# A decode step on one core: TensorE work as register loops, row slices on their own partitions, and 8 KB reads of w2 and wo

## The chip, the core and the metric

The kernel runs on one core of a Trainium2 chip. The metric is the device time of one execution in microseconds (us), lower is better. The two executions of the kernel before that are compared with the change took 104.36 and 104.44 us.

## The reference, cut to what matters

It is one token of a decoder layer with a parallel MLP: normalize the row `x` (1024), do sliding-window attention over the last 4096 cached keys, do an MLP on the normalized row, and add everything.

```python
xn = layernorm(x)                                   # x: 1 x 1024, bf16
q  = xn @ wq                                        # wq 1024 x 4096 -> 32 heads of 128
p  = softmax(q . k_window * 128**-0.5)              # 4 KV heads, window 4096, 8 query heads each
o  = p @ v_window                                   # "P.V" below
h  = gelu(layernorm(xn) @ w1 + b1)                  # w1 1024 x 3584
out = x + o @ wo + h @ w2 + b2                      # wo 4096 x 1024, w2 3584 x 1024
# (cut: the original writes these as two functions with einsum)
```

About 39.85 MB have to be read from memory for some matrix-vector products. So reading is one floor. The other is TensorE: wq, w1, w2 and wo are used as the moving operand (the one that streams past the stationary one), 512 columns at a time, 64 + 56 + 56 + 64 = 240 matmuls. A "piece" below is one of the transfers, mostly of about 1 MB, in which a matrix is read.

## The kernel before

It is a fully unrolled program. Each vector that multiplies a matrix is one stationary column, so each result is a row on one partition, spread over several banks of the accumulator. The row is copied to the on-chip memory (SBUF) and turned back into columns by one-column transposes.

```python
# q: one output row, eight banks on one partition
pe.matmul(PS[0:1, n*512:(n+1)*512], lhsT=XNTb[:, k:k+1],
          rhs=WA[:, k*NQ + n*512 : k*NQ + (n+1)*512], ...)
# ... copies of that row: 2048 columns on one partition, DVE and ACT, then 32 of these:
last = pe.matmul(PSb[:, 6*1024 + 2*h : ...+1], lhsT=Qrow[0:1, h*128:(h+1)*128],
                 rhs=identb[0:1, 0:1], is_transpose=True)
# K is transposed by TensorE (128 transposes), then 128 score matmuls of 8 columns.
# P.V: V is stationary, 8 probability columns move
for g in range(HKV):
    for b in range(NBLK):                       # 32 blocks
        pe.matmul(PS[:, 2048 + g*8 : ...+8], lhsT=V[:, (g*NBLK+b)*128 : ...+128],
                  rhs=Pb[:, (g*NBLK+b)*8 : ...+8], start=(b == 0), stop=(b == NBLK-1))
# ... w2 and wo accumulate into the same row
W2_CHUNKS = [9, 9, 8, 2]                        # rows of 2 KB per partition: runs of 18, 18, 16, 4 KB
sp.dma_start(WA[...].rearrange("p (h n) -> p h n", h=nh),      # wo: runs of 2 KB
             A_wo[h0*128:(h0+nh)*128, :].rearrange("(h d) n -> d h n", h=nh))
for h in range(32):
    for n in range(2):
        pe.matmul(PS[0:1, 3072+n*512 : ...], lhsT=OT[:, h:h+1],
                  rhs=WA[:, h*D+n*512 : ...], start=False, stop=(h == 31))
```

The order of the big reads is wq, w1, K, V, w2, wo. The matmuls of w2, P·V and wo come last.

## Time and profile before

| | before |
|---|---|
| time, median of 2 runs | 104.4 us (104.36 to 104.44) |
| span in the trace | 102.4 us |
| TensorE busy | 81.3 us |
| last wo piece landed (the trace's landing records) | 98.8 us |
| TensorE ends | 100.1 us |

The span, from the first to the last instruction of the program, is 2 us shorter than the time. First, the four rows of the page that show it in 40 slices of 2.56 us. Busy shares and clock (PEclk, the share of TensorE's full clock that was granted) are in tenths, 9 is 90% or more; GB/s is what the DMA engines moved.

```profile
PE   0021899999559998849999856489999999999991
...
PEclk9999999999999999995999955559995999999999
DMA  2999999999999999999999999999999999999910
GB/s 38 406 414 426 426 438 416 426 426 431 420 434 421 423 417 433 432 435 413 422 422 419 416 457 396 461 461 408 416 373 408 403 408 410 407 410 410 366 54 1
```

The queue is busy from the second slice to the third from last, and TensorE is at 9 in the twelve slices before the last. Where wo is read in runs of 2 KB (from about 78 us on, the 31st to 37th slice) the rate is 403 to 410 GB/s; it was 406 to 438 in the first half, apart from the first slice. The end of the chain of waits (start, duration, what; all in us) shows who closes the kernel:

```profile
43.18 23.65 DMA W<-in_B_w_dram
66.83 0.14 issue
66.96 5.34 PE PS L409 x18
...
72.37 3.30 PE PS L578 x128
...
76.00 9.98 PE PS L409 x38
85.98 12.22 PE PS L633 x56
...
98.24 1.90 PE PS L633 x8
```

Up to 66.83 us the chain is DMA; then TensorE runs w2 (L409), P·V (L578, 128 matmuls in 3.30 us) and wo (L633) without a gap to 98.20 us. Only at its last 8 matmuls does TensorE meet the last two pieces of wo, which landed at 98.2 and 98.8 us. So two limits end within 2 us of each other, and a change that relieves only one gains little.

### The profile page before, as it was taken

The page shows a single profiled execution, that of the slowest core. Times are in us where ns is not written, and L with a number is a line of the kernel's source. Part 1 is how long each engine was busy: PE and PEld are TensorE (multiplying, and loading weights), DVE is VectorE, ACT ScalarE, POOL GpSimd, SP SyncE. Part 2 cuts the span into 40 slices and gives each one's busy share as a digit, 9 for nine tenths or more (in the row PEclk, how much of TensorE's full clock was granted, in tenths as well). Part 3 has the DMA queues.
Part 4 walks back from the last instruction along what each step waited for, and adds up shares of the span by engine and source line. Part 5 has one row for each costly group of instructions (what it writes and reads, how often), then busy time and mean ns, then how long its engine had stood idle before and what let it go on. Part 6 is the DMA issues. An engine that isn't in the chain of part 4 may idle for free.

```text
span 102.4 us, 1568 instructions
## 1 busy us (share of the span) xinstructions
PE 81.3 (79%) x700; PEld 41.1 (40%) x700; DVE 22.0 (21%) x47; ACT 14.1 (14%) x16; POOL 3.5 (3%) x14
## 2 busy tenths in 40 slices
PE   0021899999559998849999856489999999999991
PEld 0020333333123331339999753023872333333320
DVE  0016400000440000074759444540110000000002
ACT  5000510000420000053337400300000000000002
POOL 5700000000000000000000000000000000000000
PEclk9999999999999999995999955559995999999999
DMA  2999999999999999999999999999999999999910
GB/s 38 406 414 426 426 438 416 426 426 431 420 434 421 423 417 433 432 435 413 422 422 419 416 457 396 461 461 408 416 373 408 403 408 410 407 410 410 366 54 1
DMA packets 8407, 39.95 MB, mean 390 GB/s; under 512 B 721, under 2 KB 721, under 8 KB 5970
## 3 DMA queue, kind: packets, MB, share of 16 engines
q1 hardware_dynamic: 8274, 39.85, 94.5%
q8 instruction: 5, 0.08, 0.3%
q0 software_dynamic: 128, 0.01, 0.1%
HBM read 39.86 MB, written 0.00 MB: 389 GB/s over the span
## 4 chain that ended last, share of the span: by engine, by line
DMA 49%; PE 34%; SPq 14%; issue 1%; DVE 1%
DMA W<-in_B_w_dram 49%; PE PS L409 15%; PE PS L633 14%; SPq L160 10%; SPq L157 4%; PE PS L578 3%; PE PS L310 2%; DVE ROW L650 1%; PE PS L588 0%; PE PS L562 0%
## 5 line engine op out<-in xcount | busy, mean ns | idle before, releaser
L409 PE MATMUL PS<-W,GT 128*1 128x512 bf16 x56 | 15.4, 443 | 1.9 <-DMA W<-in_B_w_dram 1.9
L283 PE MATMUL PS<-WA,XNTb 128*1 128x512 bf16 x64 | 16.0, 417 | 0.3 <-DVE msy L244 0.3
L310 PE MATMUL PS<-W,YTb 128*1 128x512 bf16 x56 | 12.7, 379 | 3.5 <-DVE ROW L293 2.4
L633 PE MATMUL PS<-WA,OT 128*1 128x512 bf16 x64 | 14.3, 379 | 0.0
L439 PE MATMUL PS<-identb,KV 128*128 128x128 bf16 x128 | 9.1, 243 | 1.5 <-ACT ROW L336 1.5
L409 PEld LDWEIGHTS PS<-W,GT 128*1 128x1 bf16 x56 | 5.2, 95 | 12.1 <-issue 7.3
L283 PEld LDWEIGHTS PS<-WA,XNTb 128*1 128x1 bf16 x64 | 5.7, 90 | 10.2 <-issue 2.9
L439 PEld LDWEIGHTS PS<-identb,KV 128*128 128x128 bf16 x128 | 8.8, 111 | 1.6 <-ACT ROW L336 1.6
L310 PEld LDWEIGHTS PS<-W,YTb 128*1 128x1 bf16 x56 | 4.4, 83 | 11.9 <-DVE ROW L293 2.9
L633 PEld LDWEIGHTS PS<-WA,OT 128*1 128x1 bf16 x64 | 5.2, 84 | 8.9 <-DMA WA<-in_A_wo_dram 1.0
L454 DVE COPY KV<-PS 128x1024 bf16<-128x1024 bf16 x10 | 6.3, 685 | 2.3 <-PE PS L439 2.3
L466 ACT ACTIVATE KV<-PS 128x1024 bf16<-128x1024 bf16 x6 | 5.9, 1019 | 3.3 <-PE PS L439 3.3
L650 DVE CAST ROW<-PS 1x512 bf16<-1x512 f32 x1 | 0.7, 678 | 23.6 <-PE PS L633 23.6
L293 DVE CAST ROW<-PS 1x2048 bf16<-1x2048 f32 x1 | 2.3, 2278 | 14.8 <-PE PS L283 14.8
L177 PE MATMUL PS<-identb,X 8*128 8x8 bf16 x1 | 0.2, 181 | 6.5 <-DMA X<-in_A_x_dram 6.5
L644 ACT ACTIVATE ROW<-PS 1x512 bf16<-1x512 f32 x1 | 0.6, 586 | 34.3 <-PE PS L633 34.3
L298 ACT ACTIVATE ROW<-PS 1x2048 bf16<-1x2048 f32 x1 | 1.9, 1866 | 13.8 <-PE PS L283 13.8
L480 PE MATMUL PS<-QT,KV 128*128 128x8 bf16 x128 | 3.4, 167 | 0.4 <-DVE KV L454 0.4
L480 PEld LDWEIGHTS PS<-QT,KV 128*128 128x128 bf16 x128 | 3.3, 98 | 0.6 <-DVE KV L454 0.6
L336 ACT ACTIVATE ROW<-PS 1x1536 bf16<-1x1536 f32 x1 | 1.4, 1439 | 15.3 <-PE PS L323 15.3
L331 DVE COPY QT<-PS 128x32 bf16<-128x32 bf16 x1 | 0.2, 192 | 14.8 <-PE PS L323 14.8
L578 PE MATMUL PS<-Pb,KV 128*128 128x8 bf16 x128 | 3.4, 166 | 0.0
(77 smaller groups left out, 37.8 us busy)
## 6 DMA issues: line engine op xcount, KB each, us to landing
WA<-in_A_wq_dram SPq DMA_DIRECT2D x8, 1024.0 KB, 11.7
W<-in_B_w_dram SPq DMA_DIRECT2D x8, 896.0 KB, 25.4
WA<-in_A_wo_dram SPq DMA_DIRECT2D x7, 1024.0 KB, 15.1
W<-in_B_w_dram SPq DMA_DIRECT2D x2, 2304.0 KB, 26.2
KV<-in_A_k_cache_dram SPq DMA_DIRECT2D x4, 1024.0 KB, 26.2
KV<-in_A_v_cache_dram SPq DMA_DIRECT2D x4, 1024.0 KB, 27.1
W<-in_B_w_dram SPq DMA_DIRECT2D x1, 2048.0 KB, 33.1
WA<-in_A_wo_dram SPq DMA_DIRECT2D x1, 768.0 KB, 12.7
```

Source lines behind the costliest of these rows:

```text
L157: sp.dma_start(WA[:, k * NQ:(k + 1) * NQ], A_wq[k * 128:(k + 1) * 128, :]).then_inc(s_wq[k], 16)
L160: sp.dma_start(W1[:, k * F:(k + 1) * F], B_w1[k * 128:(k + 1) * 128, :]).then_inc(s_w1[k], 16)
L283: last = pe.matmul(PS[0:1, n * 512:(n + 1) * 512], lhsT=XNTb[:, k:k + 1], rhs=WA[:, k * NQ + n * 512: k * NQ + (n + 1) * 512], start=(k == ...
L293: STATE["d_qrow0"] = DVE.mark(dve.tensor_copy(Qrow[:, 0:2048], PS[0:1, 0:2048]))
L310: last = pe.matmul(PS[0:1, (n + 1) * 512:(n + 2) * 512], lhsT=YTb[:, k:k + 1], rhs=W1[:, k * F + n * 512: k * F + (n + 1) * 512], start=(k ...
L409: pe.matmul(PS[0:1, 6 * 512 + n * 512: 6 * 512 + (n + 1) * 512], lhsT=GT[:, c:c + 1], rhs=reg[:, n * 512:(n + 1) * 512], start=False, stop ...
L439: last = pe.matmul(PSb[:, col0: col0 + 128], lhsT=KT[:, g * W + b * 128: g * W + (b + 1) * 128], rhs=identb[:, :], is_transpose=True)
L454: last = dve.tensor_copy(KT[:, g * W + (hu * 16 + 8 * s_) * 128: g * W + (hu * 16 + 8 * s_ + 8) * 128], PSb[:, bk * 1024:(bk + 1) * 1024])
L466: STATE["a_ktcopy"][u] = ACT.mark(act.activation(out=KT[:, g * W + (hu * 16 + 8) * 128: g * W + (hu * 16 + 16) * 128], in_=PSb[:, bk * 102 ...
L480: last = pe.matmul(PS[:, bank_base + b * 8: bank_base + (b + 1) * 8], lhsT=KT[:, g * W + b * 128: g * W + (b + 1) * 128], rhs=QT[:, g * 8: ...
L578: last = pe.matmul(PS[:, 4 * 512 + g * REP: 4 * 512 + (g + 1) * REP], lhsT=V[:, (g * NBLK + b) * DH:(g * NBLK + b + 1) * DH], rhs=Pb[:, (g ...
L633: last = pe.matmul(PS[0:1, 6 * 512 + n * 512: 6 * 512 + (n + 1) * 512], lhsT=OT[:, h:h + 1], rhs=WA[:, h * D + n * 512: h * D + (n + 1) * ...
```

## The change

The intent: fewer instructions and wider work outside the matrix products. A row result is no longer on one partition. For q, h and out, each 512-column slice gets its own partition: the stationary operand is a window of a zero-padded tile, so that the vector stands in column n and zeros elsewhere, and all slices accumulate in one bank. That makes the copy 512 columns wide and the turn-around four transposes instead of 32. K is transposed by VectorE, and P·V has 32 matmuls of 512 columns. w2 and wo are stored four rows per partition, so that one run is 8 KB. The TensorE program is written as loops whose addresses and waits use registers; for such a wait GpSimd counts the landed pieces of each matrix into one semaphore. The order of reads becomes wq, K, V, w1, w2, wo.

```diff
 # q (w1 likewise with YZ, 13 columns per k and 7 slices)
-    pe.matmul(PS[0:1, n*512:(n+1)*512], lhsT=XNTb[:, k:k+1], rhs=WA[...])
+    with pe.Fori(0, KC) as k:
+        pe.wait_ge(r_wq, k + 1)                  # a count that GpSimd forwards
+        for n in range(NWQ):
+            last = pe.matmul(bank(2, 512, 8),
+                lhsT=XZ[:, bass.ds(k * 15 + (7 - n), 8)],
+                rhs=WA[:, bass.ds(k * NQ + n * 512, 512)], start=False, stop=False)
 # K
-    last = pe.matmul(PSb[...], lhsT=KT[...], rhs=identb[:, :], is_transpose=True)   # x128
+    dve.transpose(KT(g).rearrange("p (b t i) -> p t b i", b=4, t=T), K(g))          # x4
 # P.V
-    last = pe.matmul(PS[..., 8 columns], lhsT=V[... 128 columns], rhs=Pb[... 8 columns])  # x128
+    with pe.Fori(0, T // 4) as t:
+        for u in range(4):
+            last = pe.matmul(
+                bank(2, 512, 32), lhsT=PT[:, bass.ds(t * 128 + u * 32, 32)],
+                rhs=Vt[:, bass.ds(t * 4 + u, 1), :, :], start=False, stop=False)
 # w2 (wo likewise with OZ, WA, r_wo and 7 passes; its eighth part stays unrolled)
-    pe.matmul(PS[0:1, ...], lhsT=GT[:, c:c+1], rhs=reg[:, n*512:(n+1)*512])
+    with pe.Fori(0, NH) as n:
+        pe.wait_ge(r_w2, n + 1)
+        for e in range(4):
+            for hf in range(2):
+                pe.matmul(bank(6, 512, 2),
+                          lhsT=GZ[:, bass.ds(n * 12 + (e * 3 + 1 - hf), 2)],
+                          rhs=W2[:, bass.ds(n * 4096 + (e * D + hf * 512), 512)],
+                          start=False, stop=False)
 # the reads
-    w2_pcn = B_w2.rearrange("(p c) n -> p c n", c=FC)        # 9, 9, 8, 2 rows a piece
+    w2_n = B_w2.rearrange("(n p e) d -> n p (e d)", p=128, e=4)
+    wo_n = A_wo.rearrange("(n p e) d -> n p (e d)", p=128, e=4)
 # (cut: set-up, layer norms, softmax with one maximum per row, gelu, forwarding on GpSimd)
```

## The prediction

> **What bounds it now.** The span is 102.4 us (the page); the measured time is 2.0 us more. In the slices all DMA engines are busy from about 2.5 to 95 us, moving 39.85 MB at 405 to 438 GB/s. The chain of waits runs over DMA to 66.8 us (w2's landing), then over TensorE without a gap to 98.2 us: 18 w2 matmuls, P·V 3.3 us, 38 w2 matmuls 9.98 us, 56 wo matmuls 12.22 us, so 218 ns per 512-column matmul at full clock. It then waits for the last wo piece, works 1.9 us, copies and stores (about 2.3 us). Queue and TensorE finish within a few us of each other. Two stretches at half clock (59 to 70 and 77 to 81 us, the clock row) cost TensorE about 3.5 us there.

> **What changes.** Bytes stay. wo goes from 2 KB to 8 KB pieces: the last slices run at 405 to 410 GB/s, the 8 KB stages at about 425; over 8.4 MB that saves about 1 us. The order becomes wq, k, v, w1, w2, wo. From before's landings (15.7 MB by 41.4 us) I put w1's last piece (24.1 MB) at 60.6 us, wo's last at 96 to 97. K is transposed on VectorE instead of TensorE[...]. Gone: one-partition copies of 2.3, 1.9 and 1.4 us, 60 one-column transposes. Scores and P·V become 32 matmuls of 512 columns each instead of 128 of 8 (3.4 us): P·V is now 7.0 us.

> **Critical path.** After h, in TensorE's order: copy and transposes, P·V (34 matmuls), w2 (56), o rearranged (estimate 2.2 us), wo (64): 154 matmuls. At 218 ns that is 33.6 us. From h ready at 62.3: 62.3+1.7+33.6+2.5 = 100.1 us, then 2.5 us to the end: span 102.6, time about 104.5, no gain, though DMA alone would allow 100.5. TensorE closes the kernel.

> **Predicted time** 107 us, 80% range 102 to 120. Faster by over 2%: 0.14; within 2%: 0.37; slower: 0.49.

> **What would show it.** DMA busy to about 96 us, then a TensorE tail of several us, wo loop without DMA waits. Start-to-start of matmuls in the w2 and wo loops: 218 is array-bound, more is sequencer-bound.[...]

> **What would make it wrong.** Loops hidden and h earlier than 61 us: 101 to 102. Register work dearer[...]: 120 or more. Half clock in the w2 loop: +3 us.

The sum under "Critical path" comes to 104.5 us; the 107 us add 2.5 us for the loops. The marked passages are cut. The time of a transpose on VectorE, and what was worked out from it, is in no term of the sum. The price of one looped matmul on the sequencer was the ground for the 2.5 us; it is the "it" of "Up to 218 it is hidden". The 1.7, 2.2 and 2.5 us of that paragraph are estimates; for o rearranged, 1.74 us (u_all) to 2.18 us (u_w2) were measured (table below).

## The result

| | before | after |
|---|---|---|
| time, median | 104.4 us | 113.44 us (113.12 to 113.76, 2 runs) |
| span | 102.4 us | 111.8 us |
| ratio, 95% interval | | 1.087 (1.079 to 1.095): slower |
| last wo piece landed | 98.8 us | 99.5 us |
| TensorE ends | 100.1 us | 109.6 us |

A ratio here and below is the mean time of one kernel's fast runs over the mean of the other's in the same rounds, so it is not quite the ratio of the medians.

The same rows of the page after (slices of 2.8 us):

```profile
PE   0279998773099563857999989888999894999992
...
PEclk9999999999656999655599999999999999999999
DMA  2999999999999999999999999999999999900000
GB/s 42 409 422 431 428 422 422 422 416 419 419 422 419 419 422 417 418 423 416 418 418 421 422 422 422 419 419 419 419 410 422 419 419 413 364 11 0 0 0 1
```

The queue is idle in the last five slices and TensorE is not: TensorE alone closes the kernel, 10 us after the last byte. That much the prediction had said. TensorE has no clock trouble in these last stages, and yet its row shows 8 where the work is dense. The groups of the page (line, engine, operation, count, busy us and mean ns of one, then idle time before them and its releaser) say where:

```profile
L340 DVE STREAM_TRANSPOSE BIG<-BIG 128x4096 bf16<-128x4096 bf16 x4 | 17.8, 4446 | 18.1 <-DMA BIG<-in_A_k_cache_dram 17.8
...
L414 PE MATMUL PS<-BIG,YZ 128*7 x56 | 14.4, 425 | 0.0
L525 PE MATMUL PS<-BIG,GZ 128*2 x56 | 13.2, 378 | 1.1 <-issue 1.1
...
L447 PE MATMUL PS<-BIG,WA 128*32 x32 | 8.9, 379 | 1.7 <-issue 1.5
```

"issue" is time in which the engine waited for nothing that the profile shows. It stands before the loops of w2 (L525) and P·V (L447), not before the loop of w1 (L414). (The mean of one matmul, 378 ns for w2, is its whole duration and overlaps the next; the time from start to start, 215 to 216 ns inside a pass of w2, is the better measure of pace.) The timeline of TensorE from P·V on, some rows of it (start, duration, what, count, idle before):

```profile
67.67 2.29 PE L447 MATMUL PS<-BIG,WA 128*32 x8
70.21 1.14 PE L447 MATMUL PS<-BIG,WA 128*32 x4 [0.25 <-issue]
71.59 1.12 PE L447 MATMUL PS<-BIG,WA 128*32 x4 [0.25 <-issue]
...
78.59 1.90 PE L525 MATMUL PS<-BIG,GZ 128*2 x8
80.65 1.89 PE L525 MATMUL PS<-BIG,GZ 128*2 x8 [0.15 <-issue]
82.76 1.89 PE L525 MATMUL PS<-BIG,GZ 128*2 x8 [0.22 <-issue]
...
95.04 12.81 PE L562 MATMUL PS<-WA,OZ 128*2 x56 [0.79 <-DVE OZ L551]
107.69 1.89 PE L572 MATMUL PS<-WA,OZ 128*2 128x512 bf16 x8
```

A pass is one run through the body of a loop; its boundary is the time from the start of its last matmul to the start of the first of the next pass. Every pass of P·V (4 matmuls) and of w2 (8 matmuls) is followed by a gap. After the first pass, the matmuls inside a pass of P·V start 245 to 270 ns apart, inside a pass of w2 or wo 215 to 216 ns apart. The boundary is 622 to 663 ns in P·V, 531 to 630 in w2 and 297 to 343 in wo. So no single price per matmul describes it.

### The profile page after: what moved, and what is told of

The parts are those of the page before. It is cut to its first block, busy times and chain, and to the rows that moved or that the text cites. A ratio compares the mean times of both kernels' runs of the same rounds, so it can differ in the third digit from the quotient of the medians.

```text
span 111.8 us, 1419 instructions
## 1 busy us (share of the span) xinstructions
PE 86.7 (78%) x346; PEld 30.6 (27%) x346; DVE 29.1 (26%) x38; ACT 10.7 (10%) x27; POOL 4.3 (4%) x20
## 3 DMA queue, kind: packets, MB, share of 16 engines
q1 hardware_dynamic: 5904, 39.85, 86.4%
## 4 chain that ended last, share of the span: by engine, by line
PE 52%; DMA 19%; DVE 18%; issue 4%; SPq 3%; ACT 2%; DVEq 0%
DMA BIG<-in_A_k_cache_dram 19%; DVE BIG L340 16%; PE PS L414 13%; PE PS L525 12%; PE PS L562 11%; PE PS L447 8%; SPq L171 3%; PE PS L352 3%; PE PS L572 2%; DVE MX L366 1%; ACT R L424 1%; ACT R L538 1%; ACT OR L580 1%; PE PS L388 1%; PE PS L356 0%
## 5 line engine op out<-in xcount | busy, mean ns | idle before, releaser
L340 DVE STREAM_TRANSPOSE BIG<-BIG 128x4096 bf16<-128x4096 bf16 x4 | 17.8, 4446 | 18.1 <-DMA BIG<-in_A_k_cache_dram 17.8
L298 PE MATMUL PS<-WA,XZ 128*8 x64 | 16.3, 414 | 1.5 <-POOLq L215 1.5
L352 PE MATMUL PS<-BIG,QBD 128*128 x32 | 11.4, 478 | 4.5 <-DVE BIG L340 3.3
L414 PE MATMUL PS<-BIG,YZ 128*7 x56 | 14.4, 425 | 0.0
L525 PE MATMUL PS<-BIG,GZ 128*2 x56 | 13.2, 378 | 1.1 <-issue 1.1
L562 PE MATMUL PS<-WA,OZ 128*2 x56 | 12.8, 378 | 0.8 <-DVE OZ L551 0.8
L447 PE MATMUL PS<-BIG,WA 128*32 x32 | 8.9, 379 | 1.7 <-issue 1.5
L298 PEld LDWEIGHTS PS<-WA,XZ 128*8 x64 | 5.8, 92 | 12.4 <-issue 6.5
L414 PEld LDWEIGHTS PS<-BIG,YZ 128*7 x56 | 5.3, 95 | 8.6 <-issue 3.1
L525 PEld LDWEIGHTS PS<-BIG,GZ 128*2 x56 | 4.6, 81 | 9.3 <-issue 4.4
L562 PEld LDWEIGHTS PS<-WA,OZ 128*2 x56 | 4.6, 82 | 8.6 <-issue 3.3
L447 PEld LDWEIGHTS PS<-BIG,WA 128*32 x32 | 2.9, 92 | 7.6 <-issue 6.7
## 6 DMA issues: line engine op xcount, KB each, us to landing
WA<-in_A_wq_dram SPq DMA_DIRECT2D x8, 1024.0 KB, 12.2
```

Source lines behind the costliest of these rows:

```text
L298: last = pe.matmul(bank(2, 512, 8), lhsT=XZ[:, bass.ds(k * 15 + (7 - n), 8)], rhs=WA[:, bass.ds(k * NQ + n * 512, 512)], start=False, stop ...
L340: dve.transpose(KT(g).rearrange("p (b t i) -> p t b i", b=4, t=T), K(g)).then_inc(S_KT, 1)
L352: last = pe.matmul(bank(hf), lhsT=QBD[:, bass.ds(k * 128, 128)], rhs=BIG[:, bass.ds(k * 1024 + (kt0 + hf * 512), 512)], start=False, stop= ...
L414: last = pe.matmul(bank(5, 512, NW1), lhsT=YZ[:, bass.ds(k * 13 + (6 - n), NW1)], rhs=W1[:, bass.ds(k * F + n * 512, 512)], start=False, s ...
L447: last = pe.matmul(bank(2, 512, 32), lhsT=PT[:, bass.ds(t * 128 + u * 32, 32)], rhs=Vt[:, bass.ds(t * 4 + u, 1), :, :], start=False, stop= ...
L525: pe.matmul(bank(6, 512, 2), lhsT=GZ[:, bass.ds(n * 12 + (e * 3 + 1 - hf), 2)], rhs=W2[:, bass.ds(n * 4096 + (e * D + hf * 512), 512)], st ...
```

## The experiments

**How the theories stood.** The main theory: TensorE's instruction sequencer, which has to run the register instructions of a loop, sets the pace where the loops are not paced by anything else. Rivals: the zero-padded operands or the shapes cost array time; the later start of P·V (67.67 us) is the loss; the half-clock stretches; the reads. "Unrolled" below means that the register loop was replaced by a loop at build time, with the same matmuls and waits on constants.

### u_all: no register loop in the TensorE program

```diff
-    with pe.Fori(0, KC) as k:            # and the five other loops likewise
+    for k in range(0, KC):
```

> All six TensorE loops written out with constant addresses, everything else as in the changed kernel. If the loops' sequencer work is what opens the end: P·V from 10.9 to about 7.4 us, w2 from 14.4 to 12.2, wo from 14.6 to 14.0, so last matmul near 103.5, span near 105.5, time near 107.2 (6 us less); h stays at 66.3 because the w1 loop already runs at 216 ns after its half-clock start. If instead the loops are hidden and only order and the wider P·V cost (rival): under 1 us changes, time 112.5 or more. If the loops also explain h's lateness: h ready before 65 us and time under 106. TensorE's program grows to some 600 instructions, so more instruction packets.

Measured: 105.61 us (105.27 to 106.48), ratio to before 1.013 (1.007 to 1.019), correct. The timeline of TensorE in the last stages:

```profile
66.03 7.08 PE L447 MATMUL PS<-BIG,WA 128*32 128x512 bf16 x32
...
73.44 12.25 PE L525 MATMUL PS<-BIG,GZ 128*2 128x512 bf16 x56
...
87.36 12.25 PE L562 MATMUL PS<-WA,OZ 128*2 128x512 bf16 x56 [0.39 <-DVE OZ L551]
99.44 1.89 PE L572 MATMUL PS<-WA,OZ 128*2 128x512 bf16 x8
```

All three products run without a gap, with the same padded operands and shapes. So the padding and the shapes cost nothing beyond the matmuls themselves, and 7.8 of the 9 us go away with the loops. That is 1.6 us more than I had expected, as much as P·V starts earlier than in after (66.03 against 67.67 us). Whether all 7.8 are the loops is a question for u_tail.

### u_pv and u_w2: one loop unrolled at a time

```diff
 # u_pv                                   # u_w2
-    with pe.Fori(0, T // 4) as t:        -    with pe.Fori(0, NH) as n:
+    for t in range(0, T // 4):           +    for n in range(0, NH):
```

> Only the P·V loop (32 matmuls, 8 passes of 4) written out. Loop theory: P·V 10.9 to 7.4 us, time about 110.0. Rival: no change.

> Only the w2 loop (7 passes of 8) written out. Loop theory: w2 14.4 to 12.2 us, the gaps of 530 to 630 ns between passes become 216, time about 111.2. Rival: no change. The wo loop's smaller gaps (300 to 340 ns) should stay if they belong to its own code; if they become 530 or more, it is where the loop lies in the instruction memory that sets them.

Measured: u_pv 108.30 us (ratio 1.037, 1.033 to 1.041), u_w2 112.13 us (1.073, 1.069 to 1.077), both correct. The times of the stages, from the first matmul of each to the first of the next, worked out from the timelines (us):

| kernel | P·V starts | P·V | w2 | o rearranged | wo, 7 of 8 parts |
|---|---|---|---|---|---|
| after | 67.67 | 10.92 | 14.30 | 2.15 | 12.65 |
| u_all | 66.03 | 7.41 | 12.18 | 1.74 | 12.08 |
| u_tail (below) | 66.04 | 7.41 | 12.18 | 1.74 | 12.08 |
| u_pv | 66.88 | 7.41 | 12.18 | 2.14 | 13.77 |
| u_w2 | 66.74 | 10.91 | 12.18 | 2.18 | 13.77 |
| pv_six (below) | 66.73 | 8.73 | 14.16 | 2.14 | 13.77 |

Two things were not plain beforehand. First, in u_pv the w2 stage is as short as unrolled although it is still a loop:

```profile
74.29 12.25 PE L525 MATMUL PS<-BIG,GZ 128*2 x56
...
88.61 13.93 PE L562 MATMUL PS<-WA,OZ 128*2 x56 [0.79 <-DVE OZ L551]
```

My reading is that the sequencer gets ahead while the static P·V runs at the array's pace, and that this lead covers all six pass boundaries of w2. pv_six (below) supports it: there P·V is still a loop, w2 starts at nearly the same moment (75.46 us), and its boundaries are 437 to 611 ns. So unrolling P·V alone took 5.6 us out of the stages up to wo (3.5 of its own, 2.1 in w2), and unrolling w2 alone only its own 2.1. Second, the wo stage became longer, in both by 1.1 us. Its matmuls show why: in u_pv the fifth to twelfth start 426 to 427 ns apart, half clock, and from the thirteenth on they start 215 to 217 ns apart, without any gap at the passes. A half-clock stretch after the pause for o costs about 1.7 us (13.77 against 12.08), and no boundary shows after it, presumably because the sequencer gets ahead during it too. Neither after nor u_all had such a stretch there. So the difference of two times alone would have misjudged both parts.

### u_tail: only the loops of P·V, w2 and wo unrolled

The edit is that of u_all, for the last three loops only. The loops of wq, scores and w1 stay.

> Only the loops of P·V, w2 and wo written out; q, scores and w1 stay loops. If the end alone matters: as u_all, 105.6. If the score loop's passes make h late as u_all's trace suggests (h at 66.0 with loops, 64.6 without): h stays at 66.0 and the time is about 1.5 us above u_all, 107.1.

Measured: 105.59 us (105.21 to 106.21), ratio 1.013 (1.008 to 1.018): the same as u_all. Its P·V starts at 66.04 us, with the loops before it still there. So the 1.64 us by which after's P·V starts later are not explained by the loops of wq, scores and w1, and the 7.8 us go away without touching them. The windows of the two traces show what they are (stretch, its length, busy time of PE, PEld, DVE, ACT, POOL with counts, then granted clock, DMA share, GB/s); first after, then u_tail, in the same three stages: scores, the maximum, w1.

```profile
31.00:48.80 17.80, 13.28 (x36) 3.63 (x36) 12.83 (x4) 0.00 (x0) 0.00 (x0) 0.79 1.01 420
48.80:51.60 2.80, 0.93 (x4) 0.62 (x4) 1.69 (x3) 0.00 (x0) 0.00 (x0) 0.50 1.00 412
51.60:66.30 14.70, 14.70 (x59) 5.43 (x59) 3.26 (x3) 1.11 (x1) 0.00 (x0) 0.85 1.02 420
```

```profile
31.00:48.80 17.80, 12.51 (x36) 3.65 (x36) 13.81 (x4) 0.00 (x0) 0.00 (x0) 0.83 1.01 418
48.80:50.40 1.60, 0.65 (x4) 0.38 (x4) 0.73 (x4) 0.00 (x0) 0.00 (x0) 1.00 1.02 421
50.40:64.30 13.90, 13.90 (x57) 5.21 (x58) 3.25 (x3) 1.11 (x1) 0.00 (x0) 0.88 1.02 419
```

The program up to there is the same and the reads are as fast. In after the clock was at a half through the whole chain of the maximum, and w1 started at 51.6 instead of 50.4 us. The clock records of after have two half-clock stretches, of 6.8 us (28.7 to 35.5 us) and 10.2 us (45.7 to 56.0 us); what decides where they fall was not shown. In the variants with loops that follow, P·V starts anywhere between 65.6 and 67.4 us. I count these 1.6 us as an accident of where the half clock fell in the profiled execution, not as a cost of the change; that is my estimate.

The equal times do not show, however, that the loop of the scores is free. In u_all a half-clock stretch (43.7 to 47.1 us) fell on the last eight score matmuls, and in u_tail none did. At full clock the two forms differ; first u_tail, with the loop, then fine_end (below), without it:

```profile
44.38 1.35 PE L352 MATMUL PS<-BIG,QBD 128*128 x4 [1.64 <-DVE BIG L340]
45.89 1.35 PE L352 MATMUL PS<-BIG,QBD 128*128 x4 [0.16 <-issue]
```

```profile
43.94 1.90 PE L353 MATMUL PS<-BIG,QBD 128*128 128x512 bf16 x8 [2.65 <-DVE BIG L341]
```

From the end of the last transpose of K to the end of the scores it is 3.75 us with the loop and 2.49 us without, so the loop costs 1.3 us there. How much of that would reach the end of the kernel at the same clock was not tested. For w1, too, nothing is shown at full clock alone: its clock is 0.85 over the stage in after, where nine of the first eleven steps from one matmul to the next are 426 to 427 ns, and 0.88 in u_tail and u_all; and after such a stretch no boundary shows in the wo of u_pv either.

### short64: the same loops with an eighth of the array work

The result is wrong: the matmuls of the three loops take 64 columns instead of 512.

```diff
-    pe.matmul(bank(6, 512, 2), lhsT=..., rhs=W2[:, bass.ds(n * 4096 + (e * D + hf * 512), 512)], ...)
+    pe.matmul(bank(6, 64, 2), lhsT=..., rhs=W2[:, bass.ds(n * 4096 + (e * D + hf * 512), 64)], ...)
     # wo likewise; P.V: bank(2, 64, 32) and rhs=Vt[:, bass.ds(t * 4 + u, 1), :, 0:16]
```

> Wrong result on purpose: P·V, w2 and wo loops stream 64 columns in place of 512, so the array no longer hides the sequencer. Start to start then is the sequencer's own cost. Loop theory: about 200 ns per matmul (fused register instruction, weight load, matmul) and 250 ns in P·V (one register instruction more), with 300 to 600 ns more once per pass, so w2 about 2.05 us a pass as before, wo 1.8 us a pass, P·V 1.38 us a pass. Rival (array or memory sets the pace): about 30 ns per matmul, passes of 0.3 to 0.5 us.

Measured (one look, state unknown): 112.64 us, against 113.44 with all columns. With an eighth of the columns in these loops the kernel takes nearly as long as with all of them: the array is not what paces these loops. (The clock was at a half from 67 to 108 us, so the array work was rather a quarter: 64 columns are about 53 ns, an estimate from the 427 ns of 512 columns at half clock. The eight unrolled matmuls at the end took 3.3 instead of 1.9 us for the same reason, so the passes are a better measure than the total.) The timeline, two passes each of P·V, w2 and wo:

```profile
68.33 0.97 PE L447 MATMUL PS<-BIG,WA 128*32 x4 [0.41 <-issue]
69.71 0.95 PE L447 MATMUL PS<-BIG,WA 128*32 x4 [0.41 <-issue]
...
80.87 1.28 PE L525 MATMUL PS<-BIG,GZ 128*2 x8 [0.83 <-issue]
83.01 1.34 PE L525 MATMUL PS<-BIG,GZ 128*2 x8 [0.86 <-issue]
...
98.34 1.31 PE L562 MATMUL PS<-WA,OZ 128*2 x8 [0.53 <-issue]
100.15 1.31 PE L562 MATMUL PS<-WA,OZ 128*2 x8 [0.49 <-issue]
```

The differences of the starts are what the sequencer needs for a pass, the first of P·V and of w2 apart: 1.36 to 1.41 us in P·V, 2.05 to 2.14 in w2, 1.80 to 1.85 in wo. With 512 columns, the trace of after shows 1.36 to 1.41, 2.05 to 2.14 and 1.80 to 1.85 as well. So the rule that fits all three loops is: a pass lasts as long as the sequencer needs for it, unless the array needs longer or the sequencer has a lead. Split by start-to-start times, one matmul of w2 or wo takes mostly 152 to 153 ns of sequencer, one of P·V 245 to 270, and the boundary of a pass is longer: 838 to 1071 ns in w2, 707 to 747 in wo, 623 to 663 in P·V. What a boundary takes beyond one matmul's price is called the head of the pass below. At full clock the array needs 8 × 216 = 1728 ns for a pass of w2 or wo, so 8 × (216 − 153) = 504 ns of head could have been hidden, and the head is larger.

### pv_six: why a matmul of P·V costs 95 ns more than one of w2

In the built program, each matmul of w2 or wo has one fused instruction of register operations ahead of it; each of P·V, but for the first of a pass, has that and a single register addition, which did not fit into the fused one. The trace of after shows both at the line of P·V (L447): 32 fused instructions, 74 ns in the median, and 24 single ones of 32 ns. To test what the single one costs, the loop of P·V counts in columns, so that six operations are enough; the result is the same.

```diff
-    with pe.Fori(0, T // 4) as t:
+    with pe.Fori(0, 897, 128) as c:
         for u in range(4):
-            ... lhsT=PT[:, bass.ds(t * 128 + u * 32, 32)], rhs=Vt[:, bass.ds(t * 4 + u, 1), :, :]
+            ... lhsT=PT[:, bass.ds(c + u * 32, 32)], rhs=Vg[:, :, bass.ds(c * 4 + u * 128, 128)]
```

> Loops kept. The P·V loop counts in columns, so both addresses of a matmul take six register operations, one fused instruction, and the single register instruction per matmul goes in three of four. Theory: that instruction is what lifts a matmul from 153 to 245-265 ns; inside a pass 216 ns (array), a pass about 1.10 us in place of 1.38, P·V about 8.8 us in place of 10.9, time about 111.3. Rival (the strided read of V or the loop's branch sets the pace): unchanged, 113.4.

Measured: 111.65 us (ratio 1.070, 1.068 to 1.072), correct. P·V is now one row of the timeline, without gaps:

```profile
66.73 8.40 PE L447 MATMUL PS<-BIG,WA 128*32 x32
```

Inside a pass the matmuls now start 215 to 216 ns apart instead of 245 to 270, and the boundary is 413 to 464 ns; the stage takes 8.73 instead of 10.92 us. So one single register instruction per matmul is what lifted P·V over the array's pace inside a pass. The stages stand in the table above; wo had its half-clock stretch, so the time fell by less than the stage did.

### pad48 and swap_v: why is a pass of w2 dearer than one of wo?

Both loops have 8 matmuls of the same form, yet w2's pass costs the sequencer 0.25 us more. Two candidates: the place of the loop in the instruction memory, and its code (w2's buffer lies at an offset, which gives its head one other register instruction than wo's: in the trace of after the seven passes show seven fused ones more than matmuls at w2's line, L525, and seven single ones of 36 ns at wo's, L562).

```diff
 # pad48, at the head of TensorE's program      # swap_v: V moved behind w1, so that W2 starts at offset 0
+    for _ in range(48):                        -    V = BIG[:, 0:HKV * W];  kt0 = HKV * W
+        pe.nop()                               +    V = BIG[:, v0:v0 + HKV * W];  kt0 = 0
```

> Loops kept; 48 empty instructions at the head of TensorE's program, while it waits for x[...]. Tells why a pass of w2 costs 2.07 us and one of wo, nearly the same code, 1.81. If the place of the loop in instruction memory does it: w2's gaps between passes fall from 530-630 to about 300 ns, or wo's rise. If its own code does it (one fused instruction of two operations where wo has a single one): both stay, time 113.4.

> Loops kept, V moved behind w1 in its buffer, so that w2's buffer starts at offset zero. That turns the second fused instruction (two operations) at the head of a w2 pass into a single register addition, as wo's loop has it, and turns the single addition in each P·V matmul into a fused one of two. If the two-operation fused instruction is the 0.27 us by which a w2 pass exceeds one of wo: w2 pass 2.07 to about 1.81 us, w2 12.7 us in place of 14.4, and P·V's matmuls rise from 245-265 ns to about 500. If a fused one of two costs about 20 ns more than a single one, P·V stays near 265 ns and w2's pass near 2.05; then that difference lies elsewhere.

Measured: pad48 113.06 us (1.084, 1.079 to 1.089), swap_v 112.39 us (1.077, 1.074 to 1.080), both correct. With 48 instructions ahead, w2's boundaries are 530 to 631 ns and wo's 297 to 342, as in after. With the same instruction sequence in both loops, w2's are still 523 to 606. Both candidates fall, the place for this one shift. (As built, swap_v also turned the single register addition of each P·V matmul into a fused instruction of two operations, and the matmuls of its undisturbed passes start 252 to 273 ns apart, against 245 to 270 in after: by these figures the fused one of two costs 3 to 7 ns more than the single addition, while that separate instruction costs about 95 (245 against the 152 to 153 of w2). A half-clock stretch fell into its P·V, so its total is no measure.)

### nowait64 and w2_last64: the wait, or the moment

Both are short64 (wrong) with one more edit. In nowait64 all pieces are waited for, by constants, before the loop, and the pass has no wait. In w2_last64 the loop of w2 is moved behind that of wo.

```diff
 # nowait64, w2 (wo likewise)                   # w2_last64
+    for q in s_w2: pe.wait_ge(q, 16)           -    (loop of w2, before the loop of wo)
     with pe.Fori(0, NH) as n:                  +    (loop of w2, after the loop of wo)
-        pe.wait_ge(r_w2, n + 1)
```

> Wrong result on purpose: short64, but w2 and wo wait for all their pieces by constants before the loop, so that no register wait stands in a pass. If the register wait makes the difference between w2 and wo: both passes then about equal, w2's extra per pass down from 850 ns to 400-580. If the wait costs nothing: w2 keeps about 850, wo about 570 ns.

> Wrong result on purpose: short64 with the w2 loop moved behind the wo loop, when the queue is idle. If the extra 270 ns per pass go with w2's loop itself: w2's pass stays near 2.05 us and wo's near 1.8 (where it does not wait for its pieces). If they go with the time (traffic of the queue or other engines' work): w2's pass falls to about 1.8 us.

Measured, one look each: 116.45 and 118.99 us; these totals say nothing, since both delay work behind all reads. The passes do. Two of w2 and one of wo in nowait64, then two of w2 in w2_last64:

```profile
83.97 1.35 PE L526 MATMUL PS<-BIG,GZ 128*2 x8 [0.42 <-issue]
85.74 1.31 PE L526 MATMUL PS<-BIG,GZ 128*2 x8 [0.42 <-issue]
...
100.55 1.30 PE L564 MATMUL PS<-WA,OZ 128*2 x8 [0.41 <-issue]
```

```profile
102.78 1.27 PE L562 MATMUL PS<-BIG,GZ 128*2 x8 [0.54 <-issue]
104.59 1.31 PE L562 MATMUL PS<-BIG,GZ 128*2 x8 [0.54 <-issue]
```

Without the wait in the pass, both loops have the same pass, 1.72 to 1.77 us in w2 and 1.70 in wo (boundaries of 629 to 700 and 619 to 620 ns), so about the array's 1.73. With the wait, it costs wo's pass about 0.1 us and w2's about 0.35. And w2's loop, when it runs last, has wo's pass, 1.80 to 1.86 us. So the dearer wait belongs to the moment, not to the loop. What at that moment makes it dearer stays open: the queue's traffic alone does not fit, because the first boundary of wo in after lies at 96.7 us, with the queue still moving data, and is 297 ns; in short64 it lies at 94 us and is 709 ns, like the later ones.

### u_early: w1's first pieces before the chain of the maximum

In after, w1's matmuls stand behind the whole maximum in TensorE's program and start at 51.6 us, although the first piece landed at 45.5 us. This variant of u_all moves three of the eight pieces into the pauses of that chain.

```diff
+    w1_part(pe, range(0, 2))                # before the transpose of the maximum
     pe.wait_ge(DVE.sem, ST["d_mx"])
     ...
+    w1_part(pe, range(2, 3))                # before the broadcast of the maximum
     pe.wait_ge(DVE.sem, ST["d_mrep"])
     ...
-    for k in range(0, KC): ...
+    w1_part(pe, range(3, KC))
```

> All loops written out as in u_all, and three of the eight w1 pieces are multiplied while VectorE works on the maximum, where TensorE idled 2.8 us. Theory (h late because TensorE reaches w1 late): h ready moves from 64.6 to about 62.8, where w1's last piece (61 to 62 us) sets it; every later step moves with it, last matmul near 100 in place of 101.1, time about 104.3. Rival (h is set by the queue already): h and time unchanged at 105.6.

Measured: 105.09 us (104.99 to 105.27), ratio 1.007 (1.006 to 1.009), correct: 0.5 us under u_all, where 1.3 had been expected. h is limited now by its last piece:

```profile
62.16 1.67 PE L365 MATMUL PS<-BIG,YZ 128*7 128x512 bf16 x7 [0.52 <-POOLq L215]
```

That piece lands at 62.1 us, while in after it landed at 60.9 us. The landing records show where the difference starts: at 38 us the trace of u_early has a 16 KB instruction packet on one DMA engine, which takes 1.06 us (that of after takes 1.07), and from there on the last of the engines ends each piece 1.7 us after the first, instead of 0.4. In after such a packet comes at 82 us for the first time (its page counts one, those of u_all and u_early two), and the same spread goes from 0.5 to 1.6 us there. So the longer unrolled program is late by about 1.2 us in the middle of the kernel; at the end both have their last landing at 99.5 to 99.6 us. (Why one packet delays its engine for good was not tested; u_all shows the same step, from 0.5 to 1.7 us, at its first packet, also at 38 us.)

### u_early_pv8 and fine_end: the versions without what was dear

u_early_pv8 puts V back as the stationary operand, 128 matmuls of 8 columns, and one part of w2 between P·V and the transpose of o. fine_end splits two of the last reads of wo into halves and waits for wo's pieces themselves instead of GpSimd's forwarded count.

```diff
 # u_early_pv8 against u_early
-    last = pe.matmul(bank(2, 512, 32), lhsT=PT[... 32 columns], rhs=Vt[... 512 columns])       # x32
+    last = pe.matmul(bank(2, 32)[:, g * REP:(g + 1) * REP],
+                     lhsT=V[:, (g * T + t) * DH:(g * T + t + 1) * DH],
+                     rhs=PT[:, t * 32 + g * REP:t * 32 + (g + 1) * REP], ...)                 # x128
 # (cut: o is then transposed once and scaled)
 # fine_end against u_early_pv8
-    pe.wait_ge(r_wo, n + 1)
+    pe.wait_ge(s_wo[n], 16)                     # parts 6 and 7: two waits, s_fin, on half pieces
```

> As u_early, and P·V with V as the stationary operand, 128 matmuls of 8 columns (3.4 us in the kernel before) in place of 32 of 512 (7.0 us). If TensorE still closed the kernel this saves 3 us or more: time near 101. If the queue closes it once the loops are gone (last piece of wo lands at 99.5 us in every run so far): time as u_early, about 104.2, with matmuls of wo waiting for their pieces. Short matmuls may bring back the half clock in w2: up to 1.7 us of TensorE, hidden by the slack.

> As u_early_pv8, with the sixth and seventh piece of wo read in halves, so that TensorE is not 16 matmuls (3.5 us) behind when the seventh piece lands at 96.6 us. Theory (queue closes the kernel, only the last pieces' size is left): last matmul 0.45 us after the last landing, near 99.6 in place of 100.3, time about 103.8, ratio to the kernel before about 0.995. Rival (more pieces cost the queue as much as they save): 104.5 or more.

Measured: u_early_pv8 104.52 us, ratio 1.002 (1.001 to 1.004); fine_end 103.99 us (103.83 to 104.10), ratio 0.997 (0.996 to 0.998); both correct. P·V takes 3.35 us instead of 7.08, but of those 3.7 us the time shows 0.6. The half-clock stretch that had been feared came right after P·V (matmuls of w2 426 to 427 ns apart), so that wo starts 2.9 us earlier; and wo now waits for its pieces, as the timelines of u_early_pv8 and then of fine_end show.

```profile
96.65 1.89 PE L574 MATMUL PS<-WA,OZ 128*2 128x512 bf16 x8 [0.60 <-POOLq L215]
98.38 1.89 PE L584 MATMUL PS<-WA,OZ 128*2 128x512 bf16 x8
```

```profile
96.78 1.03 PE L581 MATMUL PS<-WA,OZ 128*2 128x512 bf16 x4 [0.26 <-DMA WA<-in_A_wo_dram]
98.04 1.89 PE L591 MATMUL PS<-WA,OZ 128*2 128x512 bf16 x8 [0.23 <-DMA WA<-in_A_wo_dram]
```

The queue closes the kernel, with 16 matmuls of wo still behind the last whole piece in u_early_pv8; the finer end takes off 0.5 us of that. fine_end beats both kernels, though by 0.3% only over before, which is within the 2% that count as the same.

### wo_2k and w2_18k: the length of the runs

Both start from u_early_pv8, where the queue closes the kernel and so a slower read shows. wo_2k reads wo in runs of 2 KB; that permutes the rows of wo, which the comparison did not notice, presumably because attention's share of the output is too small. w2_18k reads w2 in before's pieces (18, 18, 16 and 4 KB); its result is wrong.

```diff
 # wo_2k
+    wo_o = A_wo.rearrange("(n e p) d -> n p e d", p=128, e=4)
-    sp.dma_start(WA[...], wo_n[n])
+    sp.dma_start(WA[...].rearrange("p (e d) -> p e d", e=4), wo_o[n])
 # w2_18k
+    w2_o = B_w2.rearrange("(p c) d -> p (c d)", p=128);  W2C = [0, 9, 18, 26, 28]
-    sp.dma_start(W2[:, n * 4096:(n + 1) * 4096], w2_n[n])
+    sp.dma_start(W2[:, W2C[n] * D:W2C[n + 1] * D], w2_o[:, W2C[n] * D:W2C[n + 1] * D])
```

> Wrong result on purpose: as u_early_pv8, where the queue closes the kernel, but wo read in runs of 2 KB as in the kernel before. If the 8 KB runs are worth what the traces show (2.50 us a piece of 1 MB in place of 2.56): last landing 0.5 us later, time about 105.0. Rival (run length makes no difference, the stage does): unchanged, 104.5.

> Wrong result on purpose: as u_early_pv8, but w2 read as in the kernel before, in four transfers of up to 18 KB a partition. The change made these runs shorter, not longer. If that matters as the traces show (5.44 us for 2.36 MB in place of 5.6): w2 and all of wo land 0.4 to 0.5 us earlier, time about 104.1. Rival: unchanged, 104.5.

Measured: wo_2k 106.21 us (1.018, 1.016 to 1.020), 1.7 us over u_early_pv8; w2_18k 104.06 us (0.998, 0.997 to 0.999), 0.46 under it. The slices of wo_2k show the read of wo at the end:

```profile
GB/s 29 407 426 415 441 415 437 415 428 422 419 428 412 422 431 409 423 416 424 413 427 410 429 419 425 422 409 431 419 391 386 389 386 387 386 388 386 366 45 1
```

A MB of wo took 2.71 us in 2 KB runs there, and 2.49 us in the 8 KB runs of u_early_pv8. The effect was dearer than I had expected, and dearer than in before, whose 2 KB pieces took 2.56 us; that difference is not explained. As rates, the slices in 2 KB runs show 386 to 391 GB/s in wo_2k and mostly 403 to 410 in before; the 2.49 us of the 8 KB runs are about 421, and before's 18 KB runs of w2 moved about 434 (2.36 MB in 5.44 us). For w2 the change had made the runs shorter, from 18 to 8 KB, and that cost 0.46 us by the medians (0.25 us in the last landing of the two traces, 99.10 against 98.85 us), which the prediction had not seen.

## Why the prediction was wrong

The direction and the mechanism were right; the size was not. That the measured time lies inside the range of 102 to 120 us says little, since the range reached from 2% under before to 15% over it. The forecast was 2.6 us more than before, the measurement 9.0.

**The step that failed** is the one under "The loops": "Up to 218 it is hidden. At 240 ns: +3.4 us; at 300 ns: about +15 us". It put the whole cost of a loop into one price per matmul, with 154 matmuls, and gave no price to what comes once per pass, though it had named it ("each iteration also a register wait and a branch"). The runs showed in its place:

- One matmul of w2 or wo costs 152 to 153 ns of sequencer. That is below 218 and was hidden, as the step says. The price that the forecast had put on one was too high for these 112 matmuls.
- The head of a pass is 0.55 to 0.92 us beyond one matmul's price in these two loops, and the slack of a pass of eight is 0.5 us. What is left over costs w2 2.1 us and wo 0.6.
- P·V has one more register instruction per matmul: 245 to 270 ns, and passes of only four. It costs 3.5 us, more than half of the whole, in 32 matmuls. It also takes away what hid w2's heads in u_pv (by my reading, a lead of the sequencer).
- The entry into the wo loop after o adds 0.4 us (0.79 against 0.39 us before its first matmul).

Together that is 6.6 us of loops where the central value held 2.5. The sum, worked out from the runs: u_all, without loops, is 105.6 us, where the prediction had 104.5 (+1.1); after is 7.8 us above u_all, 6.6 by the three last loops and the rest, up to 1.6 in the profiled execution, by what I take for where the half clock fell ahead of P·V (the stages differ by 8.25 us in the two traces, the medians by 7.8, since the execution that was profiled was the slower of two). So 104.5 + 1.1 + 7.8 = 113.4.

**Point by point:**

- *The queue.* w1's last piece was put at 60.6 us and landed at 60.9. wo's last was put at 96 to 97 us and landed at 99.5; "saves about 1 us" failed. The 8 KB runs do help wo (wo_2k: 1.7 us), but w2's runs became shorter (w2_18k: 0.46 us), the instruction packet at 82 us delayed wo (its second piece landed 3.61 us after the first, the next ones 2.50 us apart), and wq's pieces took 2.49 us instead of before's 2.43, for which I have no cause. It did not matter for the time, since TensorE closed the kernel, as predicted.
- *Transposes.* They took 4.45 us per group (L340 of after, 4446 ns). Four in a row ended at 44.0 us and the scores at 48.8: their loop costs 1.3 us after the last transpose (u_tail against fine_end), which the prediction had not counted, and their last matmuls ran at half clock (426 to 427 ns apart in after).
- *h.* Put at 62.3, it came at 66.3 us. The prediction took w1 to be paced by its pieces; TensorE's order held it behind the maximum until 51.6, and then it was paced by the array (14.4 us, its first matmuls at half clock). In u_all P·V starts 2.0 us later than the prediction's 64.0, from this alone. u_early got back 0.5 of it, because w1's landing is next.
- *P·V, o, w2, wo without loops.* 33.6 + 2.5 us predicted from P·V's start; u_all took 35.3 (66.03 to 101.33).
- *wq and w1 tolerate the loops.* Nothing contradicts it: u_tail, which keeps them, equals u_all. wq waits for its pieces; w1 shows no boundaries, but its clock was 0.85 over the stage in after and 0.88 in u_tail.

**What stays open:** why the register wait costs a pass of w2 0.35 us and one of wo 0.1 (about 1.5 us of the loss, w2's 2.1 less wo's 0.6); why the same 2 KB reads of wo were slower in wo_2k than in before; what fixes where the half clock falls; what the loops of scores and w1 would cost without it. None of these changes the verdict: the three last loops are the loss, and unrolled they do not lose.

## What to carry to other kernels

Price a register loop by the pass: the sequencer's time per matmul times the matmuls, plus the head (wait, branch, set-up), against the array's time of the same pass; here 8 × 153 ns plus 0.55 to 0.92 us met 8 × 216 ns. The loop of wq, whose matmuls wait for the landing pieces, cost nothing that the times show (u_tail 105.59 us with it, u_all 105.61 without), and one register instruction that does not fit into the fused one carried the loop of P·V over the array's pace (245 to 270 ns a matmul, 215 to 216 in pv_six). Look for interactions before adding up parts: behind a static P·V the loop of w2 showed no boundaries, and a half-clock stretch hid the loop of wo while it cost 1.7 us of its own.
